# Down products of a GLU block at five places of a chunk pair instead of ten, and the second block's layer-norm statistics spread over all places

## The chip, the cores and the metric

The kernel runs on one core of a Trainium2 chip. A core has a matrix engine (TensorE, PE in the profile, with its weight loads listed as PEld), VectorE (DVE), ScalarE (ACT) and GpSimd (POOL), each with its own instruction stream in a fixed order; SyncE (SP) issues transfers. Engines wait for one another through semaphores. Matmul results go to PSUM, which has eight banks of 128 x 512 floats. The metric is device time in microseconds of one execution of the whole program, as the median of several runs.

## The reference, cut to what matters

```python
x = A_x                                              # 2048 tokens x 640, fp32
h = x + irfft2(rfft2(layernorm(x)) * (w_r + 1j*w_i)) # stages one and two
z = layernorm(h)
out = h + ((z @ w_gate) * (z @ w_up)) @ w_down       # stage three: F = 1728
```

The change lies in stage three, the gated block with a hidden width of 1728.

## The kernel before, in words

**Tiling.** Tokens are taken in two blocks (`blk` 0 and 1) of 1024, each in two halves of 512 columns. The hidden width is cut into 14 chunks of 128 (`c`), two chunks making a pair (`p`). Per block the pairs run in the order 6, 0, 1, 2, 3, 4, 5: pair 6 (chunks 12 and 13) by plain products, and pairs 0 to 5 by a fast scheme that needs seven block products in place of eight (`strassen` for gate and up, `down_products` for the down projection). Every product of fp32 quality is three matmuls of split operands (high x high, high x low, low x high).

**A chunk** (`strassen(c, ...)`). Its products write three PSUM banks of a pool of four, tag `e`, handed out in turn: `oa` (new), `ob` (new), `oa` added to, `ob` added to, `oa` added to, `oc` (new), `oa` added to. In matmuls of 512 columns these are 6, 9, 6, 9, 6, 9 and 9. Three banks are taken per chunk, so the new `ob` of a chunk is the bank that was `oa` in the chunk before. After each product stands an evacuation: ScalarE copies (`h0`, L1102; `c22`, L1112; `h1`, L1119) and VectorE operations (L1122 after the second product into `ob`; L1125 and L1126 after the third into `oa`; L1132 after `oc`; L1147, which multiplies the last `oa` with `h0`, at the end). In an odd chunk VectorE has more to do after `oc`: L1134, a split (L1066), L1137 and another L1066 come ahead of L1147, and an L1066, L1158 and two more L1066 behind it. They make the operands of the pair's down products.

**Places.** Between the products stand the calls `at(1)` to `at(7)`: 1 ahead of the first product into `ob`, 2 ahead of the second into `oa`, 3 ahead of the second into `ob`, 4 ahead of the third into `oa`, 5 ahead of `oc`, 6 ahead of the fourth into `oa`, 7 behind it. What the pair before still has to do, its down products, is issued there. The instruction order of every engine is the order in which this code is written.

**Down products.** For a pair, `down_products` makes 14 products for columns 0 and 1 of the token tiles (`js`) and 14 for columns 2 and 3. Each is three matmuls of 320 columns (tile `d`) and one VectorE add into the result (L1047). Its order for two columns a and b is p1a p5a p1b | p5b p6a p3a | p6b p3b p7a | p2a p7b | p2b p4a p4b, where the bars are the five lists that it returns. The products go to four PSUM lanes (tag `d`, four banks, handed out in turn): the first lane of a column takes p1, p6, p7, p4 one after another, the second p5, p3, p2. A product on a lane has to wait until the add of the one before it on that lane has read it. The first products of columns 2 and 3 (p1, p5, p1, p5) take the four lanes anew, in the order in which the first two columns took them.

**Before the change** the ten lists stand at places 1 to 7 of the even chunk and 2, 3, 4 of the odd one, one list at each place. Pair 0 runs while pair 6's products are still to be done, and has slots of its own (four places of chunk 0, three of chunk 1).

**Layer norm of the second block.** `fill` holds 32 small operations (bn_stats L176 and L179, bn_aggr L180 and a tail, all on VectorE except one square root). They are popped at the places of the first block from chunk 1 on, behind the place's down products; whatever is left is issued ahead of chunk 6, from which the normalised tiles are made.

The lines of `strassen` and what calls it:

Of the kernel before, what the change touches and what calls it, by code (L numbers as in the profile page):

```python
# [78 lines left out]
def tile_spectral_glu(ctx: ExitStack, tc: tile.TileContext, x, wre, wim, wgu, wlast, wdown, wdlast,  # L79
# [26 lines left out]
    def single():  # L106
        return bank("e", 4)
# [4 lines left out]
    def wk(shape, name):  # L112
        return work.tile(shape, F32, tag="wk", name=name)
# [4 lines left out]
    def mmx(o, l, r, start, stop):  # L118
        nc.tensor.matmul(o, l, r, start=start, stop=stop, skip_group_check=True)  # L119
# [3 lines left out]
    def pop(n=1):  # L123
        for _ in range(n):
            if fill:
                fill.popleft()()
# [87 lines left out]
    def front(ts, k):  # L214
        n = len(ts)
        r = small.tile([P, n], F32, tag="r", name="r")
        junk = [fold[:, o:o + D] for o in (NR * 1026, NR * 1026 + D)]
        m2, ve, fs = moments(ts, junk * 2 if k < n else None, k=k)
        for i, t in enumerate(ts):
            SC[t] = r[:, i:i + 1], m2[:, i:i + 1]  # L220
        return fs, inverse_root(ve, r, n)
# [10 lines left out]
    def even(t):  # L232
        f, j = folded(t)
        fs = [(0.47, lambda: nc.vector.scalar_tensor_tensor(view(f, 0, [[321, 2], [1, 161]]),
                                                     view(XP[t], 0, [[320, 2], [1, 161]]), SC[t][1],
                                                     view(XP[t], 640, [[-320, 2], [-1, 161]]),
                                                     op0=OP.subtract, op1=OP.add))]
        fs.append((0.14, lambda: tt(j[:, 0:64], f[:, 128:192], f[:, 449:513], op=OP.add)))
        fs.append((0.4, lambda: tt(view(j, 64, [[1, 2], [2, 160]]), view(f, 161, [[-161, 2], [1, 160]]),
                                   view(f, 482, [[-161, 2], [1, 160]]), op=OP.subtract)))  # L240
        return fs
# [58 lines left out]
    for ts, when, aside, root in GROUPS:  # L300
        k = len(when)
        fs, cs = front(ts, k)
# [15 lines left out]
    for t in range(NT):  # L318
        if t == 1:
            nc.gpsimd.dma_start(frall, frem)  # L320
        if t >= 1:
            fs = even(t)
# [425 lines left out]
    def scale_shift(ts, junk, total=None):  # L748
        n = len(ts)
        r = small.tile([P, n], F32, tag="r", name="r")  # L750
        b = small.tile([P, n], F32, tag="b", name="b")
        m2, ve, fs = moments(ts, junk, total)
        cs = inverse_root(ve, r, n)
        cs.append(lambda: nc.vector.scalar_tensor_tensor(b, m2, -0.5, r, op0=OP.mult, op1=OP.mult))
        for i, t in enumerate(ts):
            SC[t] = r[:, i:i + 1], b[:, i:i + 1]
        return fs, cs
# [108 lines left out]
    for ts in (range(3), range(3, 6), range(6, 8)):  # L866
        n, t0 = len(ts), ts[-1] + 1
        fs, cs = scale_shift(ts, [scrap] * n, total[:, ts[0]:t0])
# [120 lines left out]
    def operand(sb, k):  # L989
        return xt[:, sb, k, 0], xt[:, sb, k, 1]  # L990
# [71 lines left out]
    def hi_of(src, a):  # L1062
        act(hop[:, a, 0], src, AF.Copy)  # L1063

    def lo_of(src, a, engine=nc.vector):
        engine.tensor_tensor(hop[:, a, 1], src, f32(hop[:, a, 0]), op=OP.subtract)  # L1066
# [5 lines left out]
    def strassen(c, blk, ahead, downs, side):  # L1072
        wa, ws = W[c]
        p, odd = divmod(c, 2)

        def at(n):
            if downs.get(n):
                for f in downs[n]:
                    f()
                if c:  # L1080
                    pop(2 if c in (2, 4) else 1)
            for f in side.get(n, ()):
                f()

        b11, b21, b22 = ([operand(sb, k + i) for i in range(2)] for sb, k in ((0, 0), (0, 2), (1, 2)))
        t1, t2 = ([(TJ["12"][:, 0, m, k], TJ["12"][:, 1, m, k]) for k in range(2)] for m in range(2))
        t4 = [operand(1, k) for k in range(2)]
        b5 = [operand(sb, 4) for sb in range(2)]

        def product(o, first, w, a, ms, extra=()):  # L1090
            terms = [(w, a + P * i, m) for i, m in enumerate(ms)] + list(extra)
            n = len(terms)
            for i, (w, a, m) in enumerate(terms):
                whi, wlo = w[:, 0, a:a + P], w[:, 1, a:a + P]
                mmx(o, whi, m[0], first and i == 0, False)
                mmx(o, whi, m[1], False, False)
                mmx(o, wlo, m[0], False, i == n - 1)

        oa = single()
        product(oa, True, wa, 384, b11)  # L1100
        h0 = wk([P, 512], "h0")
        act(h0, oa, AF.Copy)  # L1102
        for f in side.get(0, ()):
            f()
        if ahead and c:
            ahead[0]()
            ahead[1]()
        at(1)
        ob = single()
        product(ob, True, ws, 256, t1, [(wa, 896, b5[1])])  # L1110
        c22 = wk([P, 512], "c22")
        act(c22, ob, AF.Copy)  # L1112
        if not c:
            ahead[0]()
            ahead[1]()
        at(2)
        product(oa, False, ws, 0, t2)
        h1 = wk([P, 512], "h1")
        act(h1, oa, AF.Copy)  # L1119
        at(3)  # L1120
        product(ob, False, ws, 896, b22, [(ws, 512, b5[1])])
        tt(ob, ob, h1, op=OP.add)  # L1122
        at(4)
        product(oa, False, ws, 640, [(t3[k][:, 0], t3[k][:, 1]) for k in range(2)])
        tt(c22, oa, c22, op=OP.add)  # L1125
        tt(ob if odd else h1, ob, c22, op=OP.mult)  # L1126
        if odd:
            hi_of(ob, 2 if p < 5 else 4)
        at(5)
        oc = single()  # L1130
        product(oc, True, wa, 0, b21, [(wa, 256, b5[0])])
        tt(h0, oc, h0, op=OP.add)  # L1132
        if odd and p < 5:
            tt(oc, ob, HELD["a21"], op=OP.add)  # L1134
            hi_of(oc, 3)
            lo_of(ob, 2)
            tt(ob, ob, HELD["s3"], op=OP.subtract)  # L1137
            hi_of(ob, 4)
            lo_of(oc, 3)
        elif odd:  # L1140
            lo_of(ob, 4)
        if ahead and not odd:
            ahead[2]()
            ahead[3]()
        at(6)
        product(oa, False, wa, 640, t4, [(wa, 896, b5[0])])
        tt(oa if c == 11 else h0, oa, h0, op=OP.mult)  # L1147
        if not odd:
            HELD["a11"], HELD["a21"] = h0, h1
            if p < 5:  # L1150
                nc.gpsimd.tensor_tensor(c22, h0, h1, op=OP.subtract)
                HELD["s3"] = c22
        at(7)
        if odd and p < 5:
            hi_of(h0, 1)
            lo_of(ob, 4)
            act(oc, h0, AF.Copy)
            tt(ob, h0, ob, op=OP.subtract)  # L1158
            hi_of(ob, 6)
            lo_of(oc, 1)  # L1160
            lo_of(ob, 6)
        elif odd:
            hi_of(oa, 5)
            lo_of(oa, 5)
# [5 lines left out]
    for n, (blk, p) in enumerate(steps):  # L1170
        if p == 6:
# [121 lines left out]
            if blk == 0:  # L1293
                fs, cs = scale_shift(range(8, 16), None)
# [5 lines left out]
        slots = [{}, {}]  # L1300
        if prev[1] == 6:
            fs = [[lambda j=j, prev=prev: down(*prev, j)] for j in range(8)]
            slots = [dict(zip(range(4, 8), fs[0:3] + [fs[3] + fs[4]])), dict(zip((2, 3, 4), fs[5:]))]
        else:
            fs = down_products(*prev, (0, 1)) + down_products(*prev, (2, 3))
            slots[0] = dict(zip(range(1, 8), fs))
            slots[1] = dict(zip((2, 3, 4), fs[7:]))
        for ci in range(2):
            c = 2 * p + ci
            side = {n: [] for n in range(8)}  # L1310
# [217 lines left out]
```

## Time and profile before

| | |
|---|---|
| median of 3 runs | 674.81 us (674.58 to 676.47) |
| the profiled execution | 675.71 us |
| its span, first to last instruction | 673.9 us |
| TensorE busy | 662.8 us, 98% of the span |
| VectorE, ScalarE, GpSimd busy | 471.3, 322.7 and 393.0 us |
| chain that ended last, share of PE | 92% |
| granted TensorE clock | 1.00 |

How to read the lines below: in the timeline a row has its start, its length, the engine, the source line, the operation, output <- inputs, the shapes and how many instructions were merged; brackets hold the idle time of the engine ahead of it and what ended it. A busy table has, for a stretch, each engine's busy time. All matmuls of stages two and three go through one helper and so have the line L119: the tile name tells them apart, `e` for gate and up products, `d` for down products. A matmul's listed length (0.39 or 0.31 us) is longer than the distance to the next, since they are pipelined; the distance between starts is what counts.

### The profile page before, as it was taken

The page shows a single profiled execution, that of the slowest core. Times are in us where ns is not written, and L with a number is a line of the kernel's source. Part 1 is how long each engine was busy: PE and PEld are TensorE (multiplying, and loading weights), DVE is VectorE, ACT ScalarE, POOL GpSimd, SP SyncE. Part 2 cuts the span into 40 slices and gives each one's busy share as a digit, 9 for nine tenths or more (in the row PEclk, how much of TensorE's full clock was granted, in tenths as well). Part 3 has the DMA queues.
Part 4 walks back from the last instruction along what each step waited for, and adds up shares of the span by engine and source line. Part 5 has one row for each costly group of instructions (what it writes and reads, how often), then busy time and mean ns, then how long its engine had stood idle before and what let it go on. Part 6 is the DMA issues. An engine that isn't in the chain of part 4 may idle for free.

```text
span 673.9 us, 10264 instructions
## 1 busy us (share of the span) xinstructions
PE 662.8 (98%) x3695; PEld 588.0 (87%) x3695; DVE 471.3 (70%) x967; ACT 322.7 (48%) x622; POOL 393.0 (58%) x377
## 2 busy tenths in 40 slices
PE   7999999999999999999999999999999999999997
PEld 6999898887898888888888899898888888888887
DVE  6969896788767868584858657754747575756654
ACT  6977674585624244362626246534434252525220
POOL 3101124650298887878787544188787878787610
PEclk9999999999999999999999999999999999999999
DMA  8638975502212110042342458212002121212004
GB/s 317 225 103 258 268 223 157 179 6 78 79 40 78 40 59 25 36 115 63 92 84 79 98 116 274 79 40 68 16 34 79 40 78 40 79 40 80 1 1 156
DMA packets 48953, 66.12 MB, mean 98 GB/s; under 512 B 24082, under 2 KB 30670, under 8 KB 48774
## 3 DMA queue, kind: packets, MB, share of 16 engines
q1 hardware_dynamic: 48246, 62.91, 30.6%
q0 software_dynamic: 288, 2.16, 0.8%
q8 instruction: 29, 0.48, 0.3%
q10 hardware_dynamic: 368, 0.39, 0.3%
q14 instruction: 22, 0.18, 0.1%
HBM read 54.61 MB, written 10.84 MB: 97 GB/s over the span
## 4 chain that ended last, share of the span: by engine, by line
PE 92%; DMA 4%; DVE 2%; issue 1%; ACT 1%; SPq 0%; DVEq 0%; ACTq 0%
PE e L119 49%; PE d L119 26%; PE eo L119 4%; PE re L119 2%; PE u L455 2%; PE y L119 2%; PE im L119 2%; PE im L507 2%; DMA x<-in_x_dram 2%; PE im L252 1%; DMA bits<-in_mm_dram 1%; PE ir L507 1%; DMA wts<-in_wre_dram 1%; PE y L773 0%; SPq L155 0%
## 5 line engine op out<-in xcount | busy, mean ns | idle before, releaser
L119 PE MATMUL e<-xt,wst 128*128 128x512 f32 x864 | 213.2, 391 | 0.0
L119 PEld LDWEIGHTS e<-xt,wst 128*128 128x128 f32 x864 | 159.9, 188 | 30.5
L1047 DVE TENSOR_TENSOR x<-d,x 128x320 f32<-128x320 f32 x280 | 123.3, 483 | 51.6 <-PE d L119 47.6
L119 PE MATMUL d<-wd,ht 128*128 128x320 f32 x832 | 143.6, 309 | 0.0
L119 PEld LDWEIGHTS d<-wd,ht 128*128 128x128 f32 x832 | 131.2, 188 | 7.6
L961 POOL TENSOR_TENSOR wst<-raw,wst 128x1024 fp32r<-128x1024 f32 x23 | 55.4, 2409 | 67.2 <-ACT wst L960 49.2
L119 PE MATMUL e<-t,wst 128*128 128x512 f32 x360 | 94.4, 392 | 0.0
L119 PEld LDWEIGHTS e<-t,wst 128*128 128x128 f32 x360 | 66.3, 188 | 12.6
L119 PE MATMUL d<-wt,ht 128*128 128x320 f32 x360 | 69.5, 310 | 0.0
L977 POOL TENSOR_TENSOR wst<-raw,wst 128x896 fp32r<-128x896 f32 (+1 forms) x46 | 65.1, 1438 | 0.2 <-ACT wst L972 0.2
L119 PEld LDWEIGHTS d<-wt,ht 128*128 128x128 f32 x360 | 57.3, 188 | 2.3
L1063 ACT ACTIVATE ht<-e 128x512 fp32r<-128x512 f32 x44 | 26.4, 599 | 51.5 <-DVE e L1126 25.9
L1102 ACT ACTIVATE h<-e 128x512 f32<-128x512 f32 x24 | 14.3, 595 | 67.3 <-PE e L119 67.3
L1022 DVE TENSOR_TENSOR x<-d,x 128x320 f32<-128x320 f32 x62 | 27.5, 485 | 23.4 <-PE d L119 23.4
L658 ACT ACTIVATE wd<-draw 128x320 fp32r<-128x320 f32 (+1 forms) x30 | 15.7, 558 | 57.4 <-POOL draw L668 54.3
L972 ACT ACTIVATE wst<-raw 128x896 fp32r<-128x896 f32 (+1 forms) x48 | 30.2, 677 | 26.6 <-POOL raw L966 25.8
L119 PE MATMUL e<-xt,wdir 128*128 128x512 f32 x180 | 41.9, 392 | 0.4 <-DVE w L207 0.2
L119 PEld LDWEIGHTS e<-xt,wdir 128*128 128x128 f32 x180 | 33.5, 188 | 8.1 <-ACT xt L783 0.7
L1122 DVE TENSOR_TENSOR e<-e,h 128x512 f32<-128x512 f32 x24 | 16.8, 698 | 30.8 <-PE e L119 17.7
L1066 DVE TENSOR_TENSOR ht<-e,ht 128x512 fp32r<-128x512 f32 x54 | 36.9, 685 | 1.6 <-ACT ht L1063 1.3
L637 POOL TENSOR_TENSOR wd<-draw,wd 128x640 fp32r<-128x640 f32 x8 | 12.4, 1576 | 40.5 <-ACT wd L636 40.5
L1119 ACT ACTIVATE h<-e 128x512 f32<-128x512 f32 x24 | 14.3, 597 | 40.1 <-PE e L119 40.1
(234 smaller groups left out, 1189.5 us busy)
## 6 DMA issues: line engine op xcount, KB each, us to landing
raw<-in_wgu_dram SPq DMA_DIRECT2D x24, 640.0 KB
draw<-in_wdown_dram SPq DMA_DIRECT2D x24, 320.0 KB
wts<-in_wre_dram SPq DMA_DIRECT2D x16, 322.0 KB
x<-in_x_dram SPq DMA_DIRECT2D x15, 320.5 KB
out_dram<-x SPq DMA_DIRECT2D x15, 320.0 KB
bits<-in_mm_dram SPq DMA_DIRECT2D x32, 128.0 KB
wts<-in_wim_dram SPq DMA_DIRECT2D x9, 322.0 KB
zfar<-zr SPq DMA_DIRECT2D x32, 80.0 KB
```

Of the source, the lines that this page charges most:

```text
L119: nc.tensor.matmul(o, l, r, start=start, stop=stop, skip_group_check=True)
L507: nc.tensor.matmul(out, y[:, h, a:b], inv(g, h), start=n == 0, stop=n == len(ys) - 1)
L658: act(o[:, 0, a:a + n], src, AF.Copy)
L961: ptt(wa[:, 1], stage[:, 0:1024], f32(wa[:, 0]), op=OP.subtract)
L972: act(ws[:, 0, o:o + b - a], stage[:, a:b], AF.Copy)
L977: ptt(ws[:, 1, o:o + b - a], stage[:, a:b], f32(ws[:, 0, o:o + b - a]), op=OP.subtract)
L1022: tt(xv, ps[b][:, 0:320], xv, op=OP.add)
L1047: tt(xv, o, xv, op=OP.add)
L1063: act(hop[:, a, 0], src, AF.Copy)
L1066: engine.tensor_tensor(hop[:, a, 1], src, f32(hop[:, a, 0]), op=OP.subtract)
L1102: act(h0, oa, AF.Copy)
L1122: tt(ob, ob, h1, op=OP.add)
```

## The change

For pairs 1 to 5 of both blocks the ten lists are joined two by two, and the five runs stand at places 2, 4 and 7 of the even chunk and 2 and 4 of the odd chunk, with 6, 5, 6, 6 and 5 products. Places 1, 3, 5 and 6 of the even chunk and place 3 of the odd one hold none any more. One operation of `fill` is popped at each of the seven places of every chunk from 1 on; before, it was one or two (two in chunks 2 and 4) and only at places that held down products.

```diff
         def at(n):
-            if downs.get(n):
-                for f in downs[n]:
-                    f()
-                if c:
-                    pop(2 if c in (2, 4) else 1)
+            for f in downs.get(n, ()):
+                f()
+            if c:
+                pop()
             for f in side.get(n, ()):
                 f()
...
         else:
             fs = down_products(*prev, (0, 1)) + down_products(*prev, (2, 3))
-            slots[0] = dict(zip(range(1, 8), fs))
-            slots[1] = dict(zip((2, 3, 4), fs[7:]))
+            runs = [a + b for a, b in zip(fs[0::2], fs[1::2])]
+            slots = [dict(zip((2, 4, 7), runs)), dict(zip((2, 4), runs[3:]))]
```

## The prediction

> **What bounds the kernel now.** I read the page's engine shares and its chain first, then two tables of busy time over the stretch that the change touches, four chunk pairs of each block (215.95 to 364.23 us and 472.13 to 620.46 us).
>
> ```profile
> span 673.9 us, 10264 instructions
> ...
> PE 662.8 (98%) x3695; PEld 588.0 (87%) x3695; DVE 471.3 (70%) x967; ACT 322.7 (48%) x622; POOL 393.0 (58%) x377
> ...
> PE 92%; DMA 4%; DVE 2%; issue 1%; ACT 1%; SPq 0%; DVEq 0%; ACTq 0%
> ```
> ```profile
> sum 148.28, PE 148.28 PEld 130.25 DVE 106.87 ACT 64.68 POOL 118.89; mean PE 37.07 PEld 32.56 DVE 26.72 ACT 16.17 POOL 29.72
> ```
> ```profile
> sum 148.33, PE 148.33 PEld 130.26 DVE 94.82 ACT 59.60 POOL 118.81; mean PE 37.08 PEld 32.56 DVE 23.70 ACT 14.90 POOL 29.70
> ```
>
> In both tables the matmuls fill the whole stretch: 37.1 us per pair, no idle time. So moving a product gains nothing by covering idle PE time; the change can gain only what a matmul itself costs at a switch, and every new wait of PE adds in full. The question is which waits the down products cover now. The timeline from an odd chunk (7) to the next even one (8) answers it.
>
> ```profile
> 316.99 2.23 PE L119 MATMUL e<-xt,wst 128*128 128x512 f32 x9
> ...
> 319.05 0.60 PE L119 MATMUL d<-wd,ht 128*128 128x320 f32 x3
> ...
> 319.32 0.70 DVE L1122 TENSOR_TENSOR e<-e,h 128x512 f32<-128x512 f32 x1 [1.64 <-ACT wst L972]
> ...
> 319.93 1.28 DVE L1047 TENSOR_TENSOR x<-d,x 128x320 f32<-128x320 f32 x3
> ...
> 321.75 5.60 PE L119 MATMUL e<-xt,wst 128*128 128x512 f32 x24
> ...
> 323.99 0.69 DVE L1132 TENSOR_TENSOR h<-e,h 128x512 f32<-128x512 f32 x1 [0.61 <-PE e L119]
> ...
> 324.79 0.70 DVE L1134 TENSOR_TENSOR e<-e,h 128x512 f32<-128x512 f32 x1
> ...
> 326.59 0.68 DVE L1066 TENSOR_TENSOR ht<-e,ht 128x512 fp32r<-128x512 f32 x1
> ...
> 327.19 0.68 DVE L1147 TENSOR_TENSOR h<-e,h 128x512 f32<-128x512 f32 x1
> 327.19 1.48 PE L119 MATMUL d<-wd,ht 128*128 128x320 f32 x9
> ...
> 328.51 1.55 PE L119 MATMUL e<-t,wst 128*128 128x512 f32 x6
> 329.06 1.38 DVE L1066 TENSOR_TENSOR ht<-e,ht 128x512 fp32r<-128x512 f32 x2
> ...
> 330.35 2.07 DVE L1047 TENSOR_TENSOR x<-d,x 128x320 f32<-128x320 f32 x5
> 330.57 0.60 PE L119 MATMUL d<-wd,ht 128*128 128x320 f32 x3
> ...
> 331.01 0.64 PE L119 MATMUL d<-wt,ht 128*128 128x320 f32 x3
> ```
>
> To be seen: the 24 `e` matmuls from 321.75 are the odd chunk's place-5 and place-6 products (9 + 9) and the first product of the even chunk (6). VectorE runs behind them in an unbroken chain from L1134 to 330.44, one operation per 0.60 us, and reaches L1147, its last read of the odd chunk's bank `oa`, only at 327.19, when PE is through. What PE does in the meantime is the run of nine `d` at place 1. It ends at 328.51, after L1147 (327.87). All ten such transitions stand alike; the first and the last:
>
> ```profile
> 215.95 0.68 DVE L1147 TENSOR_TENSOR h<-e,h 128x512 f32<-128x512 f32 x1
> 215.95 0.30 PE L119 MATMUL d<-wd,ht 128*128 128x320 f32 x1
> ```
> ```profile
> 620.46 0.68 DVE L1147 TENSOR_TENSOR h<-e,h 128x512 f32<-128x512 f32 x1
> 620.47 0.31 PE L119 MATMUL d<-wd,ht 128*128 128x320 f32 x1
> ```
>
> Two latencies are needed. VectorE starts 0.20 us after PE leaves a product (the even chunk's place 7):
>
> ```profile
> 345.71 0.60 PE L119 MATMUL d<-wd,ht 128*128 128x320 f32 x3
> 345.91 0.69 DVE L1147 TENSOR_TENSOR h<-e,h 128x512 f32<-128x512 f32 x1 [1.50 <-PE e L119]
> ...
> 346.52 0.88 DVE L1047 TENSOR_TENSOR x<-d,x 128x320 f32<-128x320 f32 x2
> ```
>
> And PE after VectorE, where a lane is waited for already (product p6 on the lane of p1, whose add is the first row):
>
> ```profile
> 293.30 0.48 DVE L1047 TENSOR_TENSOR x<-d,x 128x320 f32<-128x320 f32 x1
> ```
> ```profile
> 293.47 0.60 PE L119 MATMUL d<-wd,ht 128*128 128x320 f32 x3
> 293.93 0.68 PE L119 MATMUL d<-wt,ht 128*128 128x320 f32 x3
> 294.44 0.46 PE L119 MATMUL d<-wd,ht 128*128 128x320 f32 x2
> ```
>
> Nine `d` take 1.32 us (327.19 to 328.51), so a product of three takes 0.44. The product before 294.44 therefore ran as if begun at 294.00, which is 0.22 after the add's end (293.78). Adds follow one another by 0.40 (0.88 for two of 0.48).
>
> **The change part by part.** It touches pairs 1 to 5 of both blocks (pair 0 keeps its slots): ten pairs, ten transitions into an even chunk (2, 4, 6, 8, 10).
>
> *Fewer switches.* Nine `e` behind a `d` run take 2.06 us (316.99 to 319.05), 24 in a row 5.44 (321.75 to 327.19), which is 0.2267 each or 2.04 for nine. A return to `e` thus costs 0.02, and five of ten are removed in ten pairs: 50 x 0.02 = -1.0 us. The least is 0.
>
> *Place 1 of the even chunk is emptied.* Its product `ob` then follows `oa` directly and begins a new bank. Four banks, three a chunk: it gets the odd chunk's `oa`, released by L1147. No other bank would be free sooner: the odd `ob` and `oc` are read until the chain's end. So PE waits from 327.19 to 327.87 + 0.22 = 328.09: 0.90 us, ten times, +9.0. With 0.15 (the record's start at 293.93) or 0.27 (as L1122 behind its product at 319.05) for the latency it is 8.3 to 9.5. Queued behind on PE stands the whole even chunk.
>
> *The place-2 run of six* (18 matmuls, 2.64 us) begins at 328.09 + 2.06 = 330.15. Its fifth product, p6, needs the add of the first. VectorE's chain is over at 330.44, the first product at 330.59 + 0.20, its add at 331.27; p6 could go at 331.49 and is due at 330.15 + 1.76 = 331.91. No wait, and the present ones there vanish: 0.68 or 0.64 for three matmuls in place of 0.60, ten times, 0.4 to 0.8 and with their late starts up to 1.0 in all: -0.7.
>
> *The even place 4* (p6 p3 p7 p2 p7): behind `ob` comes L1122 at +0.27, the first add at +0.88 (319.05 to 319.93) until 1.36, PE at 1.58; its fifth product is due at 1.76. Nothing. The last add is over at 2.20 + 0.20 + 0.48 = 2.88, and L1125 can only start behind six more `e`, at 2.20 + 1.38 + 0.27 = 3.85, so the emptied places 3, 5 and 6 cost nothing either: nine `e` (2.06) cover each evacuation.
>
> *Place 7* now holds p2 p4 p4 of the first two columns and p1 p5 p1 of the other two in one run. The fourth product opens a lane anew; four lanes in turn make it that of the second product (p4), two products back. L1147 starts at +0.20, the first add at +0.81, the second at +1.21 to +1.69 (345.71, 345.91, 346.52). PE goes on at 1.91, due at 3 x 0.44 = 1.32: 0.59, ten times, +5.9 (5.2 to 6.4 by the same latencies). Before, nine `e` lay between these two.
>
> *The odd place 2* (six) has VectorE idle: first add over at 1.12, wanted at 1.76. *The odd place 4* (p2 p7 p2 p4 p4): the fifth product needs the add of the second, on the same lane, which starts at 0.88 + 0.40 and ends at 1.76; PE at 1.98, due at 1.76: 0.22, ten times, +2.2 (1.5 to 2.7). From here on the odd chunk is as before, since all its down products end at this place in both, and the chain into the next even chunk starts afresh from place 5.
>
> *The layer norm's statistics.* One at each place puts them at places 5 to 7 of chunks 1 and 3, which had none there.
>
> ```profile
> 224.11 0.48 DVE L179 BATCH_NORM_STATS2 st<-x 128x6 f32<-128x320 f32 x1
> 224.51 0.47 DVE L176 BATCH_NORM_STATS2 st<-x 128x6 f32<-128x320 f32 x1
> ```
>
> The one at place 5 falls into VectorE's idle 0.61 ahead of L1132. That of place 6 stands in the chain ahead of L1147 and pushes it by 0.40: two transitions, +0.8 (0 to 1.6, if that of place 5 pushes too). Chunk 5 gets the last four at places 1 to 4, ahead of chunk 6, where they are wanted. ScalarE and GpSimd keep their operations (20.9 and 7.3 us of each pair of 37.07 are free in the first table), and no DMA is moved.
>
> *The clock.* A wait of 2.03 us in stage one left the granted clock at 1.00:
>
> ```profile
> 8.97 1.86 PE L252 MATMUL im<-bits,fold 128*128 128x128 f32 x14 [2.03 <-ACT bits L267]
> ```
> ```profile
> 6.00:10.00 4.00, 1.97 (x18) 1.00 1.03 386
> ```
>
> [...]
>
> *Sum:* 9.0 + 0.8 + 5.9 + 2.2 - 1.0 - 0.7 = **+16.2 us** (13.0 to 19.8 with all low or all high ends). The profiled execution took 675.71 us, of it 673.9 span; it would take 691.9 with a span of 690.1. It lies 0.9 above the median of the three runs, 674.81, which becomes **691.0 us**.
>
> **The rivals.**
> - *PE catches up (not slower).* An `e` takes 0.2267 for 512 columns, a `d` 0.1467 for 320: 0.417 ns a column, and 0.0133 us over in each. A pair has 192 matmuls, 2.55 us of such remainder, against 1.71 of waits. If matmuls queued behind a wait ran without it (0.0089 of each is enough), only the two gains would be left: 674.8 - 1.7 = 673.1. Against it: behind the wait at 293.93 the next two `d` take 0.46, the usual pace.
> - *The lane of place 7 is free.* If the opening product got the lane of the p2 of place 4, whose add is long done, 5.9 go: 685.1. Against it: the four lanes are handed out in turn.
> - *L1147 doesn't hold `ob`.* 9.8 go: 681.2. Against it stands that all four banks are in use at 327.19.
> - *More lane waits.* At the even place 2 the margin is 331.91 - 331.49 = 0.42. Should VectorE's chain end over 0.42 later there, ten waits of some 0.5 come: 696.
> [...]
>
> **How the numbers follow.** My forecast 0.79, PE catching up 0.03, the free lane 0.06, the free bank 0.04, more lane waits 0.06, the clock 0.02. The forecast's own range is 687.8 to 694.6; with the free lane below and the lane waits above it becomes 684.5 to 696.5, which leaves out under 2 in 10. A measurement of this kernel can tell about 0.3% (2 us) from no change: only the first rival lies within that. Slower 0.96, same 0.03, faster 0.01.
>
> **What would show it.** In the changed trace the waits of PE should name `e` of L119 behind VectorE's L1147, ten times 0.7 to 1.0, the longest two at chunks 2 and 4 of block one; a gap in the middle of each place-7 run near 0.6, and one near 0.2 before the last product of the odd place 4; each pair 1.5 us longer. I am wrong if a pair stays at 37.1, or if other waits of PE in this stage add up to more than these.

## The result, and the profile after

The changed kernel takes 685.34 us (median of six, 684.85 to 689.37) against 676.09 for the kernel before in the same runs: the ratio is 1.0147, 95% interval 1.0122 to 1.0171. That is slower, as forecast and inside the range, but by 1.5% where 2.4% was forecast. Times below are spans where nothing else is said: 673.9 us before, 683.6 after, +9.7 (forecast +16.2).

The head of the page and the chain that ended last, after:

```profile
span 683.6 us, 10287 instructions
...
PE 666.5 (97%) x3695; PEld 587.8 (86%) x3695; DVE 474.5 (69%) x967; ACT 321.7 (47%) x622; POOL 393.3 (58%) x377
...
PE 87%; DVE 9%; ACT 2%; issue 1%; DMA 1%; DVEq 0%; ACTq 0%
```

VectorE's share of the chain went from 2% to 9% although it has the same 967 instructions (474.5 us busy against 471.3): PE now stands behind it. The table of PE's waits (engine, line, releaser: total us, times, longest) names the place:

```profile
PE e L119 <- DVE h L1146: 6.4, 9, 1.1
...
PE e L119 <- DVE mv L180: 1.1, 1, 1.1
```

Ten waits at the even chunk's `ob`; the tenth is booked to a statistics operation that stands next to L1146 (L1147 before the change). The transition from chunk 7 to chunk 8 of block one, the timeline that the prediction showed of before:

```profile
365.16 3.11 PE L119 MATMUL e<-xt,wst 128*128 128x512 f32 x13
...
368.10 0.68 DVE L1146 TENSOR_TENSOR h<-e,h 128x512 f32<-128x512 f32 x1
...
368.93 1.61 PE L119 MATMUL e<-t,wst 128*128 128x512 f32 x6 [0.66 <-DVE h L1146]
...
369.97 1.37 DVE L1066 TENSOR_TENSOR ht<-e,ht 128x512 fp32r<-128x512 f32 x2
```

L1146 starts at 368.10, when PE is through with `oa` (13 matmuls of 0.2267 from 365.16), as L1147 did. The next `e` starts at 368.93. Six `e` behind other work took 1.55 and take 1.61 here; the start is 0.83 late and the rest is in the longer first matmul, some 0.90 together. The bracket's 0.66 is less because the 13 matmuls ahead are listed until 365.16 + 3.11 = 368.27, 0.17 behind the 368.10 counted here.

Place 7 of an even chunk after the change (PE, then VectorE):

```profile
270.78 0.60 PE L119 MATMUL d<-wd,ht 128*128 128x320 f32 x3
271.21 1.04 PE L119 MATMUL d<-wt,ht 128*128 128x320 f32 x6
272.09 1.48 PE L119 MATMUL d<-wd,ht 128*128 128x320 f32 x9
273.41 0.86 PE L119 MATMUL e<-xt,wst 128*128 128x512 f32 x3
```
```profile
270.98 0.69 DVE L1146 TENSOR_TENSOR h<-e,h 128x512 f32<-128x512 f32 x1 [1.35 <-PE e L119]
271.58 2.52 DVE L1047 TENSOR_TENSOR x<-d,x 128x320 f32<-128x320 f32 x6
```

Six products take 2.63 us (270.78 to 273.41), which is 18 x 0.1467: no wait, where 0.59 was forecast. VectorE is where the prediction had it (+0.20, +0.80). The fourth product starts at 272.09, but the add of the second ends only at 271.58 + 0.40 + 0.48 = 272.46. So the fourth can't write the lane of the second: lanes are not simply handed out in turn, as the text ahead of the prediction has it.

The odd place 4:

```profile
283.77 0.60 PE L119 MATMUL d<-wd,ht 128*128 128x320 f32 x3
284.21 1.21 PE L119 MATMUL d<-wt,ht 128*128 128x320 f32 x6
```

Six `d` took 1.04 before and take 1.21: 0.17 in the middle of them, forecast 0.22. All ten pairs have it, 0.15 to 0.17.

**The period of a pair.** Block two has no statistics and no normalise work, so its pairs are the cleanest measure. VectorE's operation at L1158 (another line number in other kernels) runs once a pair; the profile's entry for that line between 470 and 640 us gives the first and the last of five, four periods apart. Before and after:

```profile
L1158 DVE TENSOR_TENSOR e<-h,e x5: 685/686/686, 473.3 to 621.7; 128x512 f32<-128x512 f32 x5
```
```profile
L1157 DVE TENSOR_TENSOR e<-h,e x5: 685/685/685, 478.4 to 630.5; 128x512 f32<-128x512 f32 x5
```

37.1 and 38.0 us: +0.9 per pair. The terms: bank +0.90, odd place 4 +0.17, the old lane waits at place 2 some -0.10, fewer switches -0.09 (both worked out below); +0.88.

### The profile page after: what moved, and what is told of

It is laid out like the page before. It is cut to its first block, busy times and chain, and to the rows that moved or that the text cites. A ratio compares the mean times of both kernels' runs of the same rounds, so it can differ in the third digit from the quotient of the medians.

```text
span 683.6 us, 10287 instructions
## 1 busy us (share of the span) xinstructions
PE 666.5 (97%) x3695; PEld 587.8 (86%) x3695; DVE 474.5 (69%) x967; ACT 321.7 (47%) x622; POOL 393.3 (58%) x377
## 4 chain that ended last, share of the span: by engine, by line
PE 87%; DVE 9%; ACT 2%; issue 1%; DMA 1%; DVEq 0%; ACTq 0%
PE e L119 44%; PE d L119 26%; PE eo L119 4%; PE re L119 2%; PE u L455 2%; PE y L119 2%; PE im L119 2%; PE im L507 2%; DVE ht L1066 2%; PE im L252 2%; DVE h L1131 1%; DVE e L1133 1%; PE ir L507 1%; DVE h L1146 1%; DVE e L1136 1%
## 5 line engine op out<-in xcount | busy, mean ns | idle before, releaser
L119 PE MATMUL e<-xt,wst 128*128 128x512 f32 x864 | 210.7, 390 | 0.0
L1047 DVE TENSOR_TENSOR x<-d,x 128x320 f32<-128x320 f32 x280 | 122.9, 486 | 39.1 <-PE d L119 34.9
L119 PEld LDWEIGHTS d<-wd,ht 128*128 128x128 f32 x832 | 129.2, 188 | 4.4
L1063 ACT ACTIVATE ht<-e 128x512 fp32r<-128x512 f32 x44 | 26.4, 600 | 52.3 <-DVE e L1125 26.2
L1066 DVE TENSOR_TENSOR ht<-e,ht 128x512 fp32r<-128x512 f32 x54 | 36.9, 684 | 1.8 <-ACT ht L1063 1.3
```

What stands on the lines that cost most here:

```text
L1047: tt(xv, o, xv, op=OP.add)
```

## The experiments

The theory after the result: PE waits at `ob` of an even chunk for VectorE's last read of the odd chunk's `oa` (0.90 us); the lane wait at the odd place 4 is real; the one in place 7 is missing because the lane handed out there isn't that of the second product. The rival for the main term: long runs crowd VectorE with adds, and that is what PE pays for, wherever the runs stand. In the table, "period" is that of a pair in block two, read as above. "Stage three begins" is the start of the first matmul into a tile `e`, and its length runs from there to the start of the last matmul of the program. Up to that beginning all the kernels have the same instructions, so what differs there is not the change.

| kernel | span, us | stage three begins, us | its length, us | period, us |
|---|---|---|---|---|
| before | 673.9 | 153.4 | 516.8 | 37.1 |
| after | 683.6 | 152.7 | 527.1 | 38.0 |
| one product at place 1 | 679.6 | 153.4 | 522.3 | 37.55 |
| four at place 1 | 674.3 | 154.2 | 516.2 | 36.9 |
| fixed lanes | 688.9 | 153.2 | 531.9 | 38.5 |
| VectorE reordered | 679.1 | 154.2 | 521.1 | 37.4 |
| VectorE reordered, runs cut | 677.0 | 156.0 | 517.2 | 36.9 |
| seven at place 3 | 672.5 | 153.1 | 515.6 | 36.9 |
| pops only | 674.9 | 153.1 | 518.0 | 37.1 |
| runs only | 683.3 | 153.3 | 526.2 | 38.0 |

**One product at place 1.**

```diff
-            slots = [dict(zip((2, 4, 7), runs)), dict(zip((2, 4), runs[3:]))]
+            flat = sum(fs, [])     # runs of 1, 5, 5, 6, 6, 5 products
+            slots = [dict(zip((1, 2, 4, 7), runs)), dict(zip((2, 4), runs[4:]))]
```

> Changed kernel with the first product of the place-2 run alone at place 1. Theory (bank): 0.44 us of the 0.90 is covered, ten times: span 683.6 - 4.4 + 0.2 for one more switch = 679.4, time 681.2. Rival (crowded adds): the run at place 2 is one shorter, little changes, 685.

Measured: span 679.6, time 681.38. The timeline of PE at the same transition:

```profile
367.04 0.60 PE L119 MATMUL d<-wd,ht 128*128 128x320 f32 x3
367.86 1.40 PE L119 MATMUL e<-t,wst 128*128 128x512 f32 x5 [0.23 <-DVE h L1146]
```

The product covers its own 0.44 us and the rest of the wait stays. The crowding rival, under which little should change, fails: one early product of 28 takes back 4.0 of the 9.7 us.

**Four products at place 1.** As above, with runs of 4, 7, 6 (even places 1, 4, 7) and 8, 3 (odd places 2, 4).

> Changed kernel with its five runs of a pair cut otherwise: even chunk 4 products at place 1, 7 at place 4, 6 at place 7; odd chunk 8 at place 2, 3 at place 4. Theory (the bank that the even chunk's second product takes is held by VectorE's last read of the odd chunk, 0.90 us, ten times): four products (1.76 us) cover the wait, the fifth product's lane wait goes, and that at the odd place 4 too: span 683.6 - 9.8 - 1.7 = 672.1, time 673.9, 0.3% under the kernel before. Rival (runs of five and more products crowd their adds on VectorE, and PE waits for lanes): runs of 7 and 8 are worse, 685 or more.

Measured: span 674.3; median 675.35 against 675.65, ratio 0.9988, interval 0.9972 to 1.0005. Of the waits for L1146 and for adds none is left, with runs of seven and eight: crowding is out as the cause of the main term. The period is 36.9, under that of before:

```profile
L1157 DVE TENSOR_TENSOR e<-h,e x5: 684/685/686, 474.6 to 622.2; 128x512 f32<-128x512 f32 x5
```

The span is 2.2 over the expectation. Of that 1.5 lies ahead of stage three, which begins at 154.2 and not at 152.7 as in the changed kernel, on whose span the expectation was built (last section). Some 0.9 is in block one, mostly where the product into `ob` at place 3 waits for ScalarE's copy `c22`, which stands behind a layer-norm `normalise`; the run at place 2 had covered that.

**Seven at place 3.** The run of seven moved from place 4 to place 3, ahead of the product that waits.

> As the kernel with four products at place 1, but the run of seven stands at place 3 of the even chunk instead of place 4. Theory: it lost some 0.2 us in five even chunks of block one to a copy on ScalarE (c22, behind a normalise) that no run covered any more; a run ahead of the product that waits covers it. Span 674.3 - 1.0 = 673.3, or 672.4 where the one wait of stage two is as short as in the kernel before; time 674.2 to 675.1, up to 0.3% under the kernel before. Rival (the 2 us missing to the expectation of 672.1 are the longer runs' own cost): no change, 675.3.

Measured: median 674.43 against 675.72, ratio 0.9976, interval 0.9959 to 0.9993; span 672.5. This version is faster than both kernels, by 0.24% over the kernel before, a difference that the interval only just keeps from zero; stage three is 1.2 us shorter than before, 515.6 against 516.8. The `c22` waits are gone; some 0.2 us are left at another product of one chunk in block one.

**VectorE reordered.** PE's order is that of the changed kernel; the read of `oa` moves ahead of two other operations.

```diff
             lo_of(ob, 2)
-            tt(ob, ob, HELD["s3"], op=OP.subtract)
-            hi_of(ob, 4)
-            lo_of(oc, 3)
...
         tt(oa if c == 11 else h0, oa, h0, op=OP.mult)
+        if odd and p < 5:
+            tt(ob, ob, HELD["s3"], op=OP.subtract)
+            hi_of(ob, 4)
+            lo_of(oc, 3)
```

> Changed kernel in which VectorE does two operations of the odd chunk (L1136 and the L1066 behind it) after its last read of bank oa and not ahead of it; PE's order is that of the changed kernel. Theory (bank): the read comes 1.1 us earlier, PE doesn't wait but for 0.16 in the two even chunks with a statistics operation ahead: span 683.6 - 9.8 + 0.3 = 674.1, time 675.9. Rival (crowded adds): nothing is less crowded, 685.4.

Measured: span 679.1, 5.0 over the expectation; 1.5 of that lies ahead of stage three again. The bank wait is gone but for 0.08 in two chunks, where 0.16 was expected. A wait that I had not counted came in its place: PE reaches place 2 earlier by what it no longer waits, and the run's fifth product then stands before the first one's add.

```profile
369.64 1.92 PE L119 MATMUL d<-wd,ht 128*128 128x320 f32 x12
371.59 0.67 PE L119 MATMUL d<-wt,ht 128*128 128x320 f32 x3
```

Twelve `d` took 1.92 and the next three begin at 371.59; 12 x 0.1467 puts that at 371.40. With the longer first matmul it is 0.27 here, 0.26 to 0.33 in all eight pairs without statistics, and 0.82 and 0.87 in the two with: 4.1 together. The reordering itself added to it: from L1133 to the first add VectorE takes 5.78 us here, 5.56 before the change.

**VectorE reordered, runs cut.** The same, with runs of 4, 7, 6 at even places 2, 4, 7 and 8, 3 at odd places 2, 4, so that place 2 has no fifth product.

> The kernel with VectorE's two operations moved behind L1146, with the runs cut 4, 7, 6 (even places 2, 4, 7) and 8, 3 (odd places 2, 4). Theory (there the bank wait is gone and the next wait took its place: the fifth product of place 2 on the first one's add, 0.28 in eight pairs and 0.9 in two, 4.0 in all; and 0.17 ten times at the odd place 4): without a fifth product at place 2 both go, span 679.1 - 4.0 - 1.7 = 673.4, time 675.2, with nothing at place 1. Rival (place 1 must hold products for another reason than the bank): 679 or more.

Measured: span 677.0, time 678.77, 3.6 over the expectation, so the whole time doesn't confirm it. The period bears the theory out: 36.9 us in block two, the same as with four products at place 1, and no wait of PE in those pairs, with nothing at place 1. Block one has `c22` waits again (up to 0.5 in a chunk, 1.5 us in all). Another 1.8 lies ahead of stage three, which begins at 156.0 here and at 154.2 in the kernel that the expectation was built on: this execution had a granted clock of 0.98 in its first 100 us, and a wait of 1.9 in stage two. Stage three itself takes 517.2, 3.9 less than there.

**Fixed lanes.** Columns 2 and 3 write the very lanes of columns 0 and 1.

```diff
-            if key in ("p1", "p5"):
-                ys[j, b] = lane()
-            o = ys[j, b][:, 0:320]
+            if key in ("p1", "p5") and (j % 2, b) not in ys:
+                ys[j % 2, b] = lane()
+            o = ys[j % 2, b][:, 0:320]
...
-            fs = down_products(*prev, (0, 1)) + down_products(*prev, (2, 3))
+            ys = {}
+            fs = down_products(*prev, (0, 1), ys) + down_products(*prev, (2, 3), ys)
```

> Changed kernel in which the products of columns 2 and 3 write the very lanes of columns 0 and 1, in the same order, rather than lanes handed out anew. Theory (the predicted wait in place 7 is missing because the pool hands out the lane that was read longest ago): the fourth product of place 7 now waits for the second's add, 1.69 + 0.16 - 1.32 = 0.53, ten times: span 688.9, time 690.7. Rival (the add comes early enough for either lane): as the changed kernel, 685.4.

Measured: span 688.9, time 690.7, both as expected, with some luck: stage three is 4.8 us longer than in the changed kernel, 0.48 a pair, and it happens to begin 0.5 later. PE's waits now have ten more, and place 7 has the gap that the prediction looked for:

```profile
PE d L119 <- DVE x L1045: 2.6, 10, 0.3
```
```profile
272.22 1.04 PE L119 MATMUL d<-wt,ht 128*128 128x320 f32 x6
273.52 1.58 PE L119 MATMUL d<-wd,ht 128*128 128x320 f32 x9 [0.26 <-DVE x L1045]
```

The third run starts at 273.52, due at 272.22 + 0.88 = 273.10, and is 0.10 longer: 0.52.

**Pops only.** The kernel before with one statistics operation popped at each place.

> Kernel before (ten places), with the statistics popped one at each place as in the changed kernel. Theory: the bank wait stays covered by place 1 (L1147 ends 0.40 later, 328.27 + 0.22 against 328.51), but VectorE's chain ends 0.6 and 0.8 later in chunks 2 and 4 of block one and the fifth product's lane wait grows by that: span 673.9 + 1.4 = 675.3, time 677.1. Rival (the statistics at places 5 to 7 are a main part of the loss): 3 us or more, 679.

Measured: span 674.9. The lane wait at place 2 of chunks 2 and 4 grew by 0.40 and 0.79, the sum 1.2 against 1.4 expected. **Runs only**, the changed kernel with no statistics at places 5 to 7 of odd chunks:

> Changed kernel with no statistics popped at places 5 to 7 of odd chunks (two at places 2, 4 and 7 of chunks 2 and 4 instead). Theory: the two bank waits of 1.29 shrink to 0.90: span 683.6 - 0.8 = 682.8, time 684.6. Rival (the statistics are a main part): 3 us or more less, 682.

Measured: span 683.3, and all ten bank waits of one size:

```profile
PE e L119 <- DVE h L1146: 6.6, 10, 0.7
```

The span is only 0.3 under that of the changed kernel because stage three begins 0.6 later; stage three itself is 0.9 shorter. So the layer norm's part is some 0.8 us in the changed kernel, as forecast, and the runs are the rest.

## Why the prediction was right or wrong

- *Place 1 emptied, +9.0.* Right in mechanism and size: 0.90 us, ten times. Covering 0.44 of it gave back just that, and taking the cause away on VectorE took the wait away with PE's order unchanged.
- *Statistics, +0.8.* Right: the two waits of block one's chunks 2 and 4 are 1.29 and fall to 0.90 without them.
- *Place 7, +5.9.* This is the step that failed, and it holds nearly all of the error. "Four lanes in turn make it that of the second product" was read off the order of the code, not off a row. The time of a wait on that lane was right (0.52 with fixed lanes, 0.59 forecast); the kernel just doesn't write that lane there. The rival "the lane of place 7 is free", with 0.06, was the true case. Its 685.1 lies next to the 685.34 that came, but such closeness is partly luck, since smaller differences cancel (below). The trace fits a pool that hands out the lane whose last read was issued first: the opening product, on the lane of place 4's p2, runs free. That rule is inferred; shown is that the kernel writes another lane than the forecast assumed, and that the assumed one costs 0.5 a pair.
- *Odd place 4, +2.2.* It is there, 0.17 and not 0.22 (1.7 in all): here PE goes on 0.16 us after the add's end, not 0.22 (last section).
- *Switches, -1.0; old lane waits, -0.7.* Both are there. Pairs without waits (four products at place 1) take 36.9 against 37.08 before; less some 0.10 of lane waits, five returns to `e` cost 0.09, or 0.017 each (0.02 forecast).
- *The other rivals.* PE catches up nothing (38.0 us a pair against 37.1), L1146 does hold `ob`, and no further lane wait came at the even place 2. The chance of 0.02 for the clock was given to a fall of the clock at PE's new waits, and no run shows one: with ten such waits of 0.9 to 1.3 us in it, the changed kernel's profiled execution had a granted clock of 0.999 in the mean and of 1.00 in each of seven stretches of 77 to 100 us.
- *The rest.* 9.0 + 0.8 + 1.7 - 0.7 - 0.9 = 9.9 against 9.7. Stage three happened to begin 0.65 earlier (152.70, before 153.35; a wait of stage two, 0.8 before, is absent), so some 0.45 is left over. About 0.25 of it are longer waits of the `wdir` matmuls of pair 6; the rest stays unassigned.

## What to carry to other kernels

Work that looks like filler between two products may cover a buffer's release on another engine: ahead of emptying a slot, find the last reader of the buffer that the next product takes, and compare its end with the slot's. Take a wait away and compute the next one in line: PE arriving earlier met the next wait twice here. And which buffer a pool hands out is a fact to look up in the waits of a trace, not in the order of the code; a wait priced to 0.1 us, but on the wrong buffer, was 5.9 of the 6.5 us by which this forecast missed.

## What was not expected of the hardware

PE goes on 0.16 us after VectorE's end at the odd place 4, and 0.22 at the bank wait. At the odd place 4 the add ends at 284.66, and the weight load, for which the profile names VectorE (L1047), starts at 284.71. At the bank wait L1146 ends at 368.78, a semaphore instruction of 0.05 us stands ahead of the weight load from 368.82 to 368.87, and the weight load, for which the profile names ScalarE (L1063), starts at 368.90. What makes the difference of 0.06 was not tried. And stage two, alike in all these kernels, has one wait of PE at L455 that was absent, 0.6 to 0.8 or 1.6 to 1.9 us long in one profile or another; in four at place 1 it reads

```profile
PE u L455 <- issue: 1.7, 1, 1.7
```

so where stage three begins varies from 152.7 to 156.0 us in these profiles. Spans of single profiles are comparable no better than that, and the length of stage three or the period of a pair is the better measure. What that wait is for was not tried.
